# Two attention streams on one core: which bank a maximum is written to, and how many P @ V blocks a run takes

## Chip, core and metric

One core of a Trainium2 chip runs the whole program. The metric is the device time of one execution in microseconds (us). The kernel before was run three times: 1779.37, 1779.55 and 1779.65 us, median 1779.55. One more execution was taken with the hardware profiler: its time is 1779.57 us and its span, from the first to the last profiled instruction, 1777.8 us.

## What is computed

Cut from the reference: `x` is 2048 tokens by 512, there are 32 heads of 16 dimensions, and the second stream is cut into 4 chunks of 512 tokens.

```python
g = sigmoid((x * gate_w).sum(-1, keepdims=True))
# stream A: full softmax attention over all 2048 keys
p = softmax(einsum("bhqd,bhkd->bhqk", q, k) * Dh ** -0.5)
a = einsum("bhqk,bhkd->bhqd", p, v) @ A_wo
# stream B: causal softmax attention inside each chunk of 512, and a memory of the chunks before
for s in range(4):
    p = softmax(einsum("bhqd,bhkd->bhqk", qs, ks) * scale + mask)
    o = gb * (phi(qs) @ M) / (phi(qs) @ z + 1e-6) + (1 - gb) * (p @ vs)
    M, z = M + phi(ks).T @ vs, z + phi(ks).sum()
b = o @ B_wo
out = g * a + (1 - g) * b
```

The softmax subtracts each row's true maximum. So the kernel computes the score products twice: once to find the maxima of the rows (a "maximum"), and once more, with the maximum folded into the product as two more rows of the operands, for the exponentials.

## The kernel before

**Work and slots.** A unit is four heads of one stream against one query chunk: 32 units of A and 32 of B. In the main loop (the `while` loop from line 1019) one slot `n` is one score product of 128 keys by 512 queries; an A unit has 64 slots and a B unit 10 (`SLOTS`, line 29). The units run alternately, A then B, so that a pair has 74 slots, and there are 2368 in all.

In slot `n` the loop issues, in this order: `score_part(n)`, a score product on TensorE into one of three rotating banks of the accumulator memory (tile `st`, L744) and its exponential on ScalarE into a tile `p` (L767, L764); and then `max_part(n + 96)`, the maximum of a slot 96 places later. A maximum of A is one product into one of four banks (tiles `sm0` to `sm3`, L205), read by one VectorE reduction over 512 columns (L226). A maximum of B has, for most of its places, two products side by side in one bank, of 128 and 384 columns or of 256 and 256, and otherwise one of 512. VectorE reads each product of B with an instruction of its own that adds the causal mask (L238, with a short readback behind it). The first of two is read at once; the second waits in the list `rows_left` and is issued by `flush_rows()` when the next maximum comes, behind that one's reduction. The order of VectorE's reads is therefore B first piece, next A, B second piece, while TensorE wrote B, A.

**The bank of a maximum** is `banks[m % 4]` (L1028): the four banks in turn, whatever VectorE has read by then. A product into a bank must wait until the last read of what was there is done.

**Runs.** After every third slot (`BURST = 3`, L31) comes one run on TensorE. It is either three products of an output tile (list `shared`, L913 and L684), where any are pending, or `some_values`, which takes score blocks off a queue and multiplies them with V into the bank `ops` (L801). One block is 128 queries by four heads. Blocks of one group of four that are taken together go out as one wider product (128, 256, 384 or 512 columns); a run that crosses a group makes two. Three slots with their maxima and the run behind them are called a burst below. 74 slots are 24 2/3 bursts, so the runs fall at three different places of the units and the pattern repeats every three units, or 222 slots.

**How many blocks a run takes** is set by `most()` (L1008): normally three (`MOST`), and four when the queue is long. For A the bound falls as the unit nears its end: `64 * (len(queue) - 3) > 11 * left`, where `left` is the unit's blocks that are still to be done. A table `ends` sets the last runs of a unit. A run stops at the end of its unit. When a unit is complete its output tile is due, whose 12 products take the next four runs (`shared`); the blocks that those runs did not take have to be made up.

A pair of row maxima is transposed on TensorE in some bursts (L196, `run_late`), behind the run. The last 94 slots and what follows (`wide`) have a pattern of their own with runs after six slots; there are no maxima left by then.

Of the kernel before, what the change touches and what calls it, by code (L numbers as in the profile page):

```python
# [13 lines left out]
ALU = mybir.AluOpType  # L14
# [8 lines left out]
CH = 512  # L23
# [9 lines left out]
SLOTS = {"A": 64, "B": 10}  # L33
NU = 32
LEAD = 96
BURST = 3
LATER = (2, 3)
MOST = 3
LOW, HIGH = 3, 14
NP = 6  # L40
GAP = {"A": 2, "B": 5}
LATE_T = 9
# [5 lines left out]
def gated_mix(ctx, tc, x, xT, wqkv, a_wo, b_wq, b_wk, b_wv, b_wo, beta, gate_w, out):  # L48
    nc = tc.nc
# [54 lines left out]
    first = {}  # L104
# [5 lines left out]
    nS = len(slots)  # L110
# [64 lines left out]
    tri = {}  # L175
# [3 lines left out]
    def finish_max(u):  # L179
        nm = pmt.pop(u)  # L180
        if u[0] == "A":
            pm, nm = nm, mp.tile([128, 4, 4], F32, tag="nm", name="nm")
            nc.vector.tensor_reduce(nm, pm, axis=AX.X, op=ALU.max, negate=True)  # L183

        ms = mp.tile([128, 2, 2, 2, 4], F32R, tag="ms", name="ms")
        nv = nm.rearrange("p (r h) s -> p r h s", r=2)
        nc.gpsimd.tensor_copy(ms[:, :, 0], nv)  # L187
        nc.gpsimd.tensor_sub(ms[:, :, 1], nv, ms[:, :, 0].bitcast(F32))
        return ms
# [14 lines left out]
    def max_product(ps, u, h, s, n0, n, k, k0=0):  # L204
        nc.tensor.matmul(ps[:, n0:n0 + n], rows(qt[u][:, :, s * 128:(s + 1) * 128], h, 48), rows(k[:, :, k0:k0 + n], h, 48),  # L205
                         start=True, stop=True)

    rows_left = []

    def flush_rows():  # L210
        while rows_left:
            rows_left.pop(0)()

    def max_part(m, bank):

        u, (r, i) = maxs[m]
        side, g, c = u
        if u not in pmt:
            pmt[u] = mp.tile([128, 4, 4] + [4] * (side == "A"), F32, tag="pm" + side, name="pm")
        pm = pmt[u]  # L220
        ps = bank()
        if side == "A":

            kc, s, h = i // 8, i % 8 // 2, 2 * r + i % 2
            max_product(ps, u, h, s, 0, CH, kt_[u, kc])
            nc.vector.tensor_reduce(pm[:, h, s, kc:kc + 1], ps, axis=AX.X, op=ALU.max)  # L226
            flush_rows()
        else:


            k = kt_[u, c]
            mine = [(2 * r + h, s, 128 * (s == 2) + 256 * (s == 1 and h), 128 * (s + 1))
                    for h, s in (((0, 0), (0, 2)), ((0, 1), (1, 1)), ((1, 0), (1, 2)), ((0, 3),), ((1, 3),))[i]]
            for h, s, n0, w in mine:
                max_product(ps, u, h, s, n0, w, k)
            flush_rows()
            for h, s, n0, w in mine:
                rows_left.append(lambda h=h, s=s, n0=n0, w=w: nc.vector.tensor_tensor_reduce(  # L238
                    out=tri["rest"][:, 0:w], in0=ps[:, n0:n0 + w], in1=tri["mask"][:, CH - w:], scale=-1.0, scalar=3.0e38,
                    op0=ALU.add, op1=ALU.min, accum_out=pm[:, h, s:s + 1]))  # L240
            rows_left.pop(0)()
        if m == last_max[u]:
            def finish():

                due = min(e for e in a_last if e >= last_max[u]) + LATE_T
                late.append((min(due, first[u] + LEAD - 12), u, finish_max(u)))
            todo.append((m + 1, finish))
# [15 lines left out]
    def loads(m):  # L263

        m = min(m, len(maxs) - 1)
        while loaded[0] <= m:
            u, (r, i) = maxs[loaded[0]]
            if loaded[0] == first_max[u]:
                load_q(u)
            kc = u[2] if u[0] == "B" else i // 8  # L270
            if (u, kc) not in kt_:
                load_k(u, kc)
            loaded[0] += 1
# [350 lines left out]
    banks = [sm_ps.tile([128, CH], F32, name=f"sm{i}") for i in range(4)]  # L624
# [95 lines left out]
    wide = range(nS - LEAD + 2, nS - 4)  # L720
    assert wide.start % (2 * BURST) == wide.stop % (2 * BURST) == 0

    def from_bank(n):

        return nc.vector.tensor_copy if n > wide.start + 4 else nc.scalar.copy

    queue = []

    def score_part(n):
# [38 lines left out]
        if j % 4 == 3 or j == SLOTS[side] - 1:  # L768
            if side == "B":
# [7 lines left out]
              + [(2, 0, 256), (2, 128, 384)])  # L777

    def some_values(n, most):

        taken = len(queue)
        while queue and most and queue[0][0] <= n:
            _, u, i = queue.pop(0)
            most -= 1
            side, g, c = u
            w = 1
            while (queue and most and queue[0][0] <= n and queue[0][1] == u and (i + w) // 4 == i // 4
                   and (side == "A" or PIECES[i + w][0] == PIECES[i][0])):
                queue.pop(0)
                most -= 1  # L790
                w += 1
            p = pt_[u, i // 4]
            if side == "A":
                c0 = q0 = 128 * (i % 4)
                v = vt[u][:, i // 16, i // 4 % 4]
            else:
                b, c0, q0 = PIECES[i]
                v = vt[u][:, b]
            done = i + w == SLOTS[side]
            for h in range(4):  # L800
                nc.tensor.matmul(ops[32 * h:32 * h + 17, q0:q0 + 128 * w], v[:, 17 * h:17 * h + 17], p[:, h, c0:c0 + 128 * w],  # L801
                                 start=(i == 0), stop=done, tile_position=(0, 32 * h))
            if done:
                raw = ob.tile([128, CH], F32, tag="o", name="oraw")
                from_bank(n)(raw, ops)
                nc.sync.dma_start(od[side, c][4 * g:4 * g + 4].rearrange("h r t -> (h r) t"), raw)
                stored.add(u)
                if side == "B" and c and g % 2 == 0:
                    octet("M", g // 2, c, n + 4)
                if (side, g ^ 1, c) in stored and u != ("A", NG - 1, NCH - 1):  # L810
                    octet(side, g // 2, c, n + (20 if side == "B" and (g < 5 or c < last) else 8))
                if u in between:
                    shared.extend(output(*between[u]))
                if side == "A" and c == 0:
                    shared.extend(later_tile(LATER[g // NO], g % NO))
                break
        return taken - len(queue)
# [117 lines left out]
    def output(c, b, pairs, then, ps=ops):  # L935

        ks = [(os, o, i) for os in pairs for o in os for i in range(2)]
        for k in ks:
            def f(n, k=k):
                os, o, i = k  # L940
                assert loaded_blocks[c, b, os] > len(blocks) - 2
                t = blocks[loaded_blocks[c, b, os] - 1][:, i, o % 2].unsqueeze(1)
                list(products(ps, t, 0, "AB"[i], o, k == ks[0], k == ks[-1]))[n]()
                if k == ks[-1] and n == 2:
                    then(ps, c, b)
            for n in range(3):
                yield lambda n=n, f=f: f(n)
# [57 lines left out]

    ends = {"A": {9: 3, 8: 4, 7: 3, 6: 3, 5: 5}, "B": {10: 3, 7: 3, 4: 4}}

    def most():  # L1008

        if not queue:  # L1010
            return 0
        side = queue[0][1][0]
        left = SLOTS[side] - queue[0][2]
        over = 64 * (len(queue) - LOW) > (HIGH - LOW) * (left if side == "A" else 0)
        return ends[side].get(left, MOST + over)

    filled = [0]
    n = 0
    while n < nS or queue or beside or filled[0] < len(fill):
        for f in beside.pop(n, []):  # L1020
            f()
        if n < nS:
            score_part(n)
        m = n + LEAD
        if m < nS:
            loads(m + PRE)

            max_part(m, lambda: banks[m % 4])  # L1028
        run_todo(m)
        if n >= nS or n % (2 * BURST if n in wide else BURST) == (2 * BURST if n in wide else BURST) - 1:  # L1030
            taken = 0
            if shared:
                for _ in range(3):
                    shared.pop(0)()
            else:
                taken = some_values(n, 8 if n >= nS or n in wide else most())
            if n < 5:


                for i in range(4):  # L1040
                    nc.tensor.matmul(ops[:, 128 * i:128 * i + 128], identf, identf, start=True, stop=True)
            if any(e[0] < m + 1 for e in late):
                run_late(st_ps, "st", m + 1)
            else:

                for _ in range(0 if n >= nS and queue else 4 if n not in wide else 11 - taken if taken < 8 else 0):
                    if filled[0] == len(fill) or fill[filled[0]][0] > n:
                        break
                    fill[filled[0]][1]()
                    filled[0] += 1  # L1050
        n += 1
# [45 lines left out]
```

## Time and profile before

| | |
|---|---|
| median of three runs | 1779.55 us (1779.37 to 1779.65) |
| profiled execution | 1779.57 us, span 1777.8 us |
| TensorE (PE) busy | 1770.5 us, 100% |
| weight loads (PEld) busy | 915.2 us, 51% |
| VectorE (DVE) busy | 1573.5 us, 89% |
| ScalarE (ACT) busy | 1435.4 us, 81% |
| GpSimd (POOL) busy | 641.2 us, 36% |

The projections take the first 302 us or so; the main loop's bursts with maxima run from there to 1702 us; the last stage ends at 1778 us. Matmuls are pipelined and their ends are modelled, so that a matmul which streams behind another still counts as busy: PE at 100% says little by itself. In the rows of the timeline the columns are the start in us, the length in us, the engine, the line, the operation, the tiles written and read, and how many instructions in a row were merged (x8). Where two follow each other with an overlap, the merged length runs from the first start to the last end.

### The profile page before, as it was taken

The numbers are of one execution on the slowest core, as the hardware profiler recorded it, in microseconds if no ns is written. First come the engines' busy times: TensorE is split into PE (matmuls) and PEld (weight loads), VectorE is DVE, ScalarE is ACT, GpSimd is POOL, SyncE is SP. The second block draws the span as 40 slices with busy tenths as digits, with TensorE's granted clock in tenths as the row PEclk, the third lists the DMA queues.
The fourth block names the chain that finished last, engine by engine and source line by source line (L and its number), as shares of the span: only waits on it lengthen the run. The fifth ranks groups of instructions, "written<-read, shape, count | busy, mean of one in ns | idle before, by whom it ended". The sixth has DMA issues, their size and how long they took to land.

```text
span 1777.8 us, 40673 instructions
## 1 busy us (share of the span) xinstructions
PE 1770.5 (100%) x14945; PEld 915.2 (51%) x14945; DVE 1573.5 (89%) x3331; ACT 1435.4 (81%) x2752; POOL 641.2 (36%) x748
## 2 busy tenths in 40 slices
PE   9999999999999999999999999999999999999999
PEld 8887776444444444444444444444444444444444
DVE  4236777999999999999999999999999999999931
ACT  5455445888888888888888888888888888888884
POOL 3002223415161417443434343344434253435343
PEclk9999999999999999999999999999999999999999
DMA  7667566445453536555454544454545353544542
GB/s 251 212 234 239 182 205 187 121 110 134 128 152 107 147 108 179 143 146 128 132 143 121 145 127 146 128 146 126 147 112 154 113 141 116 150 119 138 144 160 62
DMA packets 141270, 261.55 MB, mean 147 GB/s; under 512 B 36328, under 2 KB 58888, under 8 KB 140560
## 3 DMA queue, kind: packets, MB, share of 16 engines
q1 hardware_dynamic: 139712, 257.55, 50.3%
q8 instruction: 119, 1.95, 0.5%
q0 software_dynamic: 1216, 1.14, 0.3%
q14 instruction: 79, 0.65, 0.1%
q10 hardware_dynamic: 144, 0.26, 0.0%
HBM read 174.39 MB, written 83.25 MB: 145 GB/s over the span
## 4 chain that ended last, share of the span: by engine, by line
PE 95%; DVE 1%; ACT 1%; DMA 1%; POOL 1%; issue 0%; SPq 0%; POOLq 0%; DVEq 0%
PE ops L801 33%; PE st L744 27%; PE sm L205 14%; PE pr L311 10%; PE ops L913 4%; PE ops L684 2%; PE sm L913 2%; PE num L514 1%; POOL mn L378 1%; PE pr L401 1%; PE mps L545 0%; DVE pm L226 0%; DMA qdB<-q 0%; PE mt_ps L196 0%; DMA raw<-xT 0%; PE sm L744 0%
## 5 line engine op out<-in xcount | busy, mean ns | idle before, releaser
L767 ACT ACTIVATE p<-st 128x512 f32<-128x512 f32 x2261 | 1189.5, 601 | 152.3 <-PE sm L205 108.2
L226 DVE TENSOR_REDUCE pm<-sm 128x1 f32<-128x512 f32 x2048 | 1281.1, 683 | 11.5 <-PE sm L205 11.3
L744 PE MATMUL st<-qA,kA 50*128 50x512 f32 x2014 | 663.4, 432 | 0.0
L205 PE MATMUL sm<-kA,qA 48*128 48x512 f32 x2048 | 660.4, 428 | 0.4
L801 PE MATMUL ops<-p,vA 128*17 128x128 f32 (+3 forms) x6432 | 552.0, 442 | 0.0
L744 PEld LDWEIGHTS st<-qA,kA 50*128 50x128 f32 x2014 | 328.0, 185 | 415.1 <-ACT p L767 370.6
L205 PEld LDWEIGHTS sm<-kA,qA 48*128 48x128 f32 x2048 | 331.7, 185 | 16.9 <-issue 4.6
L863 POOL TENSOR_TENSOR rcp<-rec,minus 128x32 f32<-128x32 f32 x43 | 234.2, 5446 | 76.4 <-DMA rec<-dend 71.8
L238 DVE CUSTOM_DVE_ANT_0 rest<-sm,mask 128x128 f32<-128x128 f32 (+3 forms) x512 | 247.3, 483 | 1.4
L801 PEld LDWEIGHTS ops<-p,vA 128*17 128x17 f32 x6432 | 130.5, 96 | 214.4 <-issue 189.4
L748 POOL TENSOR_SCALAR_AFFINE_SELECT p<-p 128x512 f32<-128x512 f32 x128 | 79.4, 636 | 324.9 <-ACT p L767 320.4
L205 PE MATMUL sm<-kB,qB 48*128 48x128 f32 (+3 forms) x512 | 166.2, 385 | 0.0
L744 PE MATMUL st<-qB,kB 50*128 50x512 f32 (+1 forms) x495 | 109.3, 330 | 0.3 <-ACT mt L199 0.3
L381 DVE TENSOR_TENSOR q<-full,q 128x512 fp32r<-128x512 f32 x56 | 38.6, 689 | 74.9 <-ACT q L374 67.9
L744 PEld LDWEIGHTS st<-qB,kB 50*128 50x128 f32 x495 | 69.9, 186 | 59.3 <-ACT p L767 48.6
L801 PE MATMUL ops<-p,vB 128*17 128x128 f32 (+3 forms) x1504 | 87.5, 350 | 0.0
L205 PEld LDWEIGHTS sm<-kB,qB 48*128 48x128 f32 x512 | 80.0, 184 | 0.0
L187 POOL CAST ms<-nm 128x16 fp32r<-128x16 f32 x32 | 6.3, 196 | 201.5 <-DVE nm L183 199.6
L378 POOL TENSOR_SCALAR mn<-full 128x512 f32<-128x512 f32 x24 | 36.4, 1515 | 102.5 <-ACT full L373 82.2
L373 ACT COPY full<-pr 128x512 f32<-128x512 f32 x56 | 32.8, 586 | 40.2 <-PE pr L311 37.3
L187 POOL CAST ms<-pm 128x16 fp32r<-128x16 f32 x32 | 6.3, 196 | 127.9 <-DVE pm L238 127.8
L801 PEld LDWEIGHTS ops<-p,vB 128*17 128x17 f32 x1504 | 33.1, 97 | 31.1 <-issue 26.6
(198 smaller groups left out, 1622.7 us busy)
## 6 DMA issues: line engine op xcount, KB each, us to landing
kA<-kdA SPq DMA_DIRECT2D x256, 128.0 KB
vA<-vdA SPq DMA_DIRECT2D x31, 544.0 KB
kA<-kdA SPq DMA_DIRECT2D x256, 64.0 KB
kdA<-q SPq DMA_DIRECT2D x32, 256.0 KB
qdB<-q SPq DMA_DIRECT2D x32, 256.0 KB
qA<-qdA SPq DMA_DIRECT2D x64, 128.0 KB
kdB<-q SPq DMA_DIRECT2D x32, 256.0 KB
qB<-qdB SPq DMA_DIRECT2D x64, 128.0 KB
```

The source lines that it names most:

```text
L205: nc.tensor.matmul(ps[:, n0:n0 + n], rows(qt[u][:, :, s * 128:(s + 1) * 128], h, 48), rows(k[:, :, k0:k0 + n], h, 48), start=True, stop=True)
L226: nc.vector.tensor_reduce(pm[:, h, s, kc:kc + 1], ps, axis=AX.X, op=ALU.max)
L238: rows_left.append(lambda h=h, s=s, n0=n0, w=w: nc.vector.tensor_tensor_reduce(out=tri["rest"][:, 0:w], in0=ps[:, n0:n0 + w], in1=tri["mas ...
L311: nc.tensor.matmul(ps, l(a, k), r(b, k), start=(n == 0), stop=(n == 11))
L378: nc.gpsimd.tensor_scalar_min(ph["mn"], full, 0.0)
L381: nc.vector.tensor_sub(q2, full, q1.bitcast(F32))
L744: nc.tensor.matmul(ps[:, n0:n0 + CH - q0], rows(k[:, :, b * 128:(b + 1) * 128], h, 50), rows(q[:, :, q0:], h, 50), start=True, stop=True)
L748: nc.gpsimd.affine_select(out=x, in_=x, pattern=[[0, 4], [1, 128]], base=0, channel_multiplier=-1, compare_op=ALU.is_ge, fill=0.0)
L767: nc.scalar.activation(p[:, h], ps, AF.Exp, scale=SCALE)
L801: nc.tensor.matmul(ops[32 * h:32 * h + 17, q0:q0 + 128 * w], v[:, 17 * h:17 * h + 17], p[:, h, c0:c0 + 128 * w], start=(i == 0), stop=done ...
L863: eng.tensor_tensor(r, rec, minus, op=ALU.pow)
L913: yield lambda i=i, x=x, w=w: nc.tensor.matmul(ps, t[:, b, x], halved[side][:, o, w], start=start and i == 0, stop=stop and i == 2)
```

## The change

Two things are changed together. First, the bank of a maximum: instead of `banks[m % 4]` the loop takes the bank whose last read stands earliest in VectorE's order. A counter numbers the reads as they are issued, and `oldest()` takes the bank with the lowest number; a read of a second piece of B renews the number of its bank.

Second, `most(n)` decides between three and four blocks from what is left: `runs` is the number of runs up to the place where the unit's last blocks become due, and a run takes four where the blocks left, less four, are at least 3.5 times the runs left, provided that more than six blocks are there to take before the next run (`due`), or that it is the last. For B, and behind the end of a unit, the table `ends` still holds, with four where more than three blocks are queued.

```diff
-LOW, HIGH = 3, 14
+LOW = 3
...
+    read_last = dict(zip(range(4), range(4)))
+    def oldest():
+        return min(read_last, key=read_last.get)
+    def was_read(b):
+        if b is not None:
+            read_last[b] = count[0] = count[0] + 1
+    count = [4]
-    def max_part(m, bank):
+    def max_part(m, bank, b=None):
...
             nc.vector.tensor_reduce(pm[:, h, s, kc:kc + 1], ps, axis=AX.X, op=ALU.max)
+            was_read(b)
             flush_rows()
...
+            if b is not None:
+                read_last[b] = 9 * nS
...
+            def masked(h, s, n0, w):
+                nc.vector.tensor_tensor_reduce(
...
+                was_read(b)
             for h, s, n0, w in mine:
-                rows_left.append(lambda h=h, s=s, n0=n0, w=w: nc.vector.tensor_tensor_reduce(
...
+                rows_left.append(lambda h=h, s=s, n0=n0, w=w: masked(h, s, n0, w))
...
-    def most():
+    def most(n):
         if not queue:
             return 0
-        side = queue[0][1][0]
-        left = SLOTS[side] - queue[0][2]
-        over = 64 * (len(queue) - LOW) > (HIGH - LOW) * (left if side == "A" else 0)
-        return ends[side].get(left, MOST + over)
+        _, u, done = queue[0]
+        side, left = u[0], SLOTS[u[0]] - done
+        runs = (first[u] + SLOTS[side] + GAP[side] + 1 - n) // BURST
+        if side == "B" or runs < 1:
+            return ends[side].get(left, MOST + (len(queue) > LOW))
+        due = min(SLOTS[side], (n + BURST - GAP[side] - first[u] + 1) // 4 * 4) - done
+        return MOST + (left - 4 >= (MOST + 0.5) * runs and (due > 2 * MOST or runs == 1))
...
-            max_part(m, lambda: banks[m % 4])
+            b = oldest()
+            max_part(m, lambda: banks[b], b)
...
-                taken = some_values(n, 8 if n >= nS or n in wide else most())
+                taken = some_values(n, 8 if n >= nS or n in wide else most(n))
```

More of the change, by code (lines that the diff above doesn't have):

```diff
@@ L236, in max_part @@
             flush_rows()
+            def masked(h, s, n0, w):
+                nc.vector.tensor_tensor_reduce(
+                    out=tri["rest"][:, 0:w], in0=ps[:, n0:n0 + w], in1=tri["mask"][:, CH - w:], scale=-1.0, scalar=3.0e38,
+                    op0=ALU.add, op1=ALU.min, accum_out=pm[:, h, s:s + 1])
+                was_read(b)
             for h, s, n0, w in mine:
-                rows_left.append(lambda h=h, s=s, n0=n0, w=w: nc.vector.tensor_tensor_reduce(
-                    out=tri["rest"][:, 0:w], in0=ps[:, n0:n0 + w], in1=tri["mask"][:, CH - w:], scale=-1.0, scalar=3.0e38,
-                    op0=ALU.add, op1=ALU.min, accum_out=pm[:, h, s:s + 1]))
+                rows_left.append(lambda h=h, s=s, n0=n0, w=w: masked(h, s, n0, w))
             rows_left.pop(0)()
```

## The prediction

> **What bounds the kernel now.** I read the busy times by stage first, then the timeline of VectorE, then that of TensorE. One window is 222 slots, three units of each stream; the fence has two of them.
>
> ```profile
> core 0: us, PE busy (x) PEld busy (x) DVE busy (x) ACT busy (x) POOL busy (x), PEclk, DMA share, GB/s
> ...
> 889.64:1026.28 136.64, 136.64 (x1283) 63.00 (x1286) 136.45 (x292) 120.88 (x235) 51.71 (x59) 1.00 0.50 136
> ...
> 1436.20:1572.85 136.65, 136.65 (x1284) 63.05 (x1286) 136.49 (x292) 120.91 (x235) 51.71 (x59) 1.00 0.52 136
> ```
>
> VectorE is busy for 136.45 of 136.64 us, and ScalarE for 120.88. TensorE's 136.64 says little, since a matmul that streams behind another counts as busy. VectorE's own busy time hides something too, which its timeline shows.
>
> ```profile
> 860.25 4.87 DVE L226 TENSOR_REDUCE pm<-sm 128x1 f32<-128x512 f32 x8
> 865.11 0.69 DVE L238 CUSTOM_DVE_ANT_0 rest<-sm,mask 128x512 f32<-128x512 f32 x1
> 865.73 0.08 DVE L238 DVE_READ_ACCUMULATOR2_ANT pm<- 128x1 f32 x1
> 865.73 1.28 DVE L226 TENSOR_REDUCE pm<-sm 128x1 f32<-128x512 f32 x2
> 867.00 0.69 DVE L238 CUSTOM_DVE_ANT_0 rest<-sm,mask 128x512 f32<-128x512 f32 x1
> ...
> 867.62 9.31 DVE L226 TENSOR_REDUCE pm<-sm 128x1 f32<-128x512 f32 x15
> 876.84 0.21 DVE L183 TENSOR_REDUCE nm<-pm 128x16 f32<-128x64 f32 x1
> 876.97 3.07 DVE L226 TENSOR_REDUCE pm<-sm 128x1 f32<-128x512 f32 x5
> 880.13 0.29 DVE L238 CUSTOM_DVE_ANT_0 rest<-sm,mask 128x128 f32<-128x128 f32 x1
> 880.35 0.08 DVE L238 DVE_READ_ACCUMULATOR2_ANT pm<- 128x1 f32 x1
> ...
> 882.83 0.55 DVE L238 CUSTOM_DVE_ANT_0 rest<-sm,mask 128x384 f32<-128x384 f32 x1
> 883.30 0.08 DVE L238 DVE_READ_ACCUMULATOR2_ANT pm<- 128x1 f32 x1
> ...
> 887.49 0.42 DVE L238 CUSTOM_DVE_ANT_0 rest<-sm,mask 128x256 f32<-128x256 f32 x1
> 887.83 0.08 DVE L238 DVE_READ_ACCUMULATOR2_ANT pm<- 128x1 f32 x1
> ...
> 890.66 4.40 DVE L226 TENSOR_REDUCE pm<-sm 128x1 f32<-128x512 f32 x7
> ```
>
> Eight reductions take 4.87 us and two take 1.28. So the step from one to the next is (4.87 - 1.28) / 6 = 0.598 us, one alone takes 1.28 - 0.60 = 0.68, and each overlaps the one before it by 0.08 us. A delay of less than 0.08 us between two reads leaves no idle time in any view; it shows only as a group longer than its steps. The 15 reductions from 867.62 should take 14 x 0.598 + 0.68 = 9.05 us and take 9.31: 0.26 us were lost. The seven at 890.66 should take 4.27 and take 4.40: 0.13 lost.
>
> VectorE's work in a window, at its own pace: 192 reductions x 0.598 = 114.8 us; B's masked reads by width, from the starts of the reads and their readbacks, 0.21, 0.34, 0.47 and 0.62 us (880.13 to 880.35, 887.49 to 887.83, 882.83 to 883.30, 865.11 to 865.73), four of each for a unit, three units, 19.7 us; the small reduction at 876.84 takes 0.13 before the next starts, three times, 0.4 us. Sum 134.9. The window lasts 136.64, so about 1.7 us of it, 1.3%, is VectorE waiting for TensorE. That is all the change can win back here: 9.8 windows lie between 360 and 1702 us, 17 us in all.
>
> **Where it is lost.** TensorE's bursts, first score to first score:
>
> ```profile
> 868.31 0.50 PE L744 MATMUL st<-qA,kA 50*128 50x512 f32 x1
> ...
> 870.20 0.50 PE L744 MATMUL st<-qA,kA 50*128 50x512 f32 x1
> ...
> 872.08 0.50 PE L744 MATMUL st<-qA,kA 50*128 50x512 f32 x1
> ...
> 873.76 0.49 PE L744 MATMUL st<-qA,kA 50*128 50x512 f32 x1
> ...
> 875.66 0.50 PE L744 MATMUL st<-qA,kA 50*128 50x512 f32 x1
> ```
> ```profile
> 925.39 0.50 PE L744 MATMUL st<-qA,kA 50*128 50x512 f32 x1
> ...
> 927.22 0.39 PE L196 MATMUL mt_ps<-identf,ms 128*32 128x128 f32 x4
> 927.54 0.50 PE L744 MATMUL st<-qA,kA 50*128 50x512 f32 x1
> ...
> 929.25 0.50 PE L744 MATMUL st<-qA,kA 50*128 50x512 f32 x1
> ...
> 931.05 0.49 PE L744 MATMUL st<-qA,kA 50*128 50x512 f32 x1
> ```
>
> A burst with a run of four blocks takes 1.89 us (868.31 to 870.20), with three blocks 1.68 (872.08 to 873.76), with four in two products 1.90 (873.76 to 875.66), with four and the transposed maxima 2.15 (925.39 to 927.54). VectorE needs 3 x 0.598 = 1.79 us for three reads of A, and with a B among them 1.82 (0.62 + 1.20) or 1.88 (two pieces, 0.68 + 1.20). So beside A alone a four makes TensorE 0.10 us later and a three 0.11 earlier; beside a B a four costs 0.01 to 0.07 and a three gains 0.14 to 0.20. TensorE has a reserve of a few tenths, since the banks are filled ahead; a row of fours eats it, and then each further one is lost time on VectorE.
>
> I followed `most()` through the loop slot by slot, for the old and the new rule. The runs of an A unit behind the four shared runs and the three of B (T: with transposed maxima):
>
> old: I 4444444 3 444 3T33 444; II 4344433443444T332 44; III 443444344434 3T433 2 4
> new: I 444444444 3 4 3T33 444; II 443434343434 3T433 44; III 443434343434 3T4343 4
>
> Each sums to 64 blocks. I, II and III are the three places at which runs fall in a unit. The rows above are of a unit I: the delays at 865.11 and 867.00 (0.08 and 0.07 against the 0.598 steps before them) and the 0.26 stand in its seven fours, the 0.17 ahead of 880.13 (876.97 + 5 x 0.598 = 879.96) at its T, the 0.13 of 890.66 behind its last three. Sum 0.71. For II and III:
>
> ```profile
> 912.10 10.32 DVE L226 TENSOR_REDUCE pm<-sm 128x1 f32<-128x512 f32 x17
> ...
> 927.38 0.68 DVE L226 TENSOR_REDUCE pm<-sm 128x1 f32<-128x512 f32 x1
> 928.13 0.29 DVE L238 CUSTOM_DVE_ANT_0 rest<-sm,mask 128x128 f32<-128x128 f32 x1
> ```
> ```profile
> 958.10 9.93 DVE L226 TENSOR_REDUCE pm<-sm 128x1 f32<-128x512 f32 x16
> 967.94 0.21 DVE L183 TENSOR_REDUCE nm<-pm 128x16 f32<-128x64 f32 x1
> 968.07 4.27 DVE L226 TENSOR_REDUCE pm<-sm 128x1 f32<-128x512 f32 x7
> 972.34 0.29 DVE L238 CUSTOM_DVE_ANT_0 rest<-sm,mask 128x128 f32<-128x128 f32 x1
> ```
>
> II loses 0.07 in its 17 reductions (10.25 at their pace) and 0.15 ahead of 928.13, behind the four with a T: 0.22. III loses 0.28 in 16 (9.65) and 0.08 ahead of 972.34: 0.36. These rows name 1.29 of the 1.7; the other 0.4 is in spots of some 0.05 each.
>
> **The change part by part.** *The runs.* Unit I gets two more fours in its row: 2 x 0.10 = 0.20 lost more. Ahead of its T there is now a 3 and a 4 in place of a 3 and three fours, 0.20 less, against the 0.17 lost there; I take 0.07 saved, as its reserve starts from nothing. I: 0.13 worse (bounds 0 and 0.20). Unit II alternates fours and threes, +0.10 and -0.11, so the reserve stays, and its T stands behind a three, 0.21 us shorter: all 0.22 is saved. Unit III alternates too: 0.28 and half of the 0.08, 0.32 saved. Of the unnamed 0.4 I take a quarter, 0.10 (bounds 0 and 0.4). Sum -0.13 + 0.22 + 0.32 + 0.10 = 0.51 a window, times 9.8: **5.0 us**. There are 9 fewer products of A in all (804 and 795 pieces); by 1.89 against 1.90 that is 0.1 us, nothing. The queue gets up to two blocks longer at some places, so that a `p` tile is released a run later; ScalarE's idle time covers that (120.88 of 136.64 busy). If that cover were gone, the next exponential, and through its score bank the next score, would stand a run late.
>
> *The banks.* What differs is the order behind a B of two pieces: the next burst's second maximum no longer waits for the second piece, its third does, at the same moment as the second did. One spot a window shows such a wait in full:
>
> ```profile
> 980.40 0.50 PE L205 MATMUL sm<-kB,qB 48*128 48x256 f32 x2
> 980.74 0.40 PE L744 MATMUL st<-qB,kB 50*128 50x512 f32 x1
> 981.13 0.50 PE L205 MATMUL sm<-kA,qA 48*128 48x512 f32 x2
> ```
> ```profile
> PEld st L744 <- ACT p L767: 419.3, 809, 0.9
> ...
> PEld sm L205 <- DVE pm L238: 4.0, 13, 0.5
> ```
>
> The product at 981.13 could stand beside the score at 980.74: 0.39 us. It comes where TensorE is ahead, and the whole list names 4.0 us of such waits against 419.3 for ScalarE's score banks, which take over as the limit. So between 0 and 0.39 a window; nearer to 0, since reserve that TensorE gains while it is ahead is used only by the next row of fours: 0.04, **0.4 us** in all. Behind the moved wait stand the burst's third product, its run and the next score; they waited there already. The counter and the choice are made when the program is built, no engine runs them; DMAs, SP's and POOL's queues keep their order.
>
> Forecast: 1779.57 - 5.0 - 0.4 = **1774.2 us** against the profiled execution's own time, of which 1.8 lies around the span; the median of the runs is 0.02 less, so nothing is to be converted. Its own range, by the bounds of I and of the unnamed spots, is 1770 to 1776.5.
>
> **The rivals.**
>
> *More is won.* The banks free TensorE behind each two-piece B, and the whole 0.39 becomes reserve that unit I uses: another 0.35 x 9.8 = 3.4 us, 1770.8. For it: unit I's losses are still there to win. Against it: the 419.3 us of the score banks.
>
> *VectorE is full.* What looks like lost steps is the reads' own scatter, and only the idle 0.19 us of a window (136.64 - 136.45) can be won: 1.9 us, 1777.7, not to be told from no change. For it: the busy share. Against it: the groups of 4.87 and of 9.31 have the same step but for the fours beside them. The Trainium skill, Perfetto Trace Analysis, Identifying the Most-Contended Engine, says that occupancy is a fair measure of VectorE's closeness to its limit; by that rule the time would be this one, and the overlapping groups of the trace speak against it. To this case I add the one that delays only move along, from II and III into the next unit's start.
>
> *Slower: the threes don't repay.* A three that waits for a score bank gains nothing: 929.25 to 931.05 is one of 1.80 us. If the threes between the fours are all like this, a pair costs 1.89 + 1.80 against 3.59, 0.10 lost, six pairs each in II and III: 1.2 a window, in place of the 0.58 that II and III lose by the rows above. Worse by 0.62 x 9.8 = 6.1 us, 1785.7. It decides from a mean of 1.70 us for these threes (3.59 - 1.89). Against it: the three behind a row of fours took 1.68.
>
> **How the numbers follow.** What a measurement here can tell from no change is 0.2%, 3.6 us: faster is below 1776.0. Chances: forecast 0.52, more won 0.16, VectorE full 0.23, threes don't repay 0.09. Faster takes the second whole and most of the first, 0.64; same the 0.23 and the forecast's upper end, 0.27; slower 0.09. The range 1769 to 1779.5 holds the first three cases but for their edges; the slower one is left out.
>
> **What would show it.** Each window shorter by about 0.5 us; in units II and III groups of reductions at the 0.598 step, with no 9.93 for 16; in unit I the long group of its fours longer than today's by 0.2 us. The wait at 981.13 gone. It is wrong if the threes in II and III take 1.75 us or more, or if unit I's row costs more than II and III give back.

## The result and the profile after

The changed kernel takes 1772.95 us (median of six runs, 1772.17 to 1773.54); the kernel before, run beside it, 1779.72 us (1779.37 to 1781.19). The ratio is 0.9961, with an interval of 0.9951 to 0.9971: faster by 6.8 us. The profiled execution has a span of 1771.8 us; before it was 1777.8.

One window of 222 slots in the timeline by stretches, from the first maximum of one unit I to that of the next; columns as before:

```profile
core 0: us, PE busy (x) PEld busy (x) DVE busy (x) ACT busy (x) POOL busy (x), PEclk, DMA share, GB/s
855.11:991.02 135.91, 135.91 (x1277) 62.32 (x1274) 135.87 (x292) 120.88 (x235) 58.93 (x67) 1.00 0.49 136
```

The same work takes 135.9 us where it took 136.6. VectorE's 134.9 us of work are unchanged, so it now waits 1.0 us and not 1.7. VectorE's timeline of the changed kernel, units I, II and III one after the other (the reduction is at L238 now and the masked read at L253):

```profile
858.39 4.87 DVE L238 TENSOR_REDUCE pm<-sm 128x1 f32<-128x512 f32 x8
...
865.73 9.50 DVE L238 TENSOR_REDUCE pm<-sm 128x1 f32<-128x512 f32 x15
...
875.27 3.07 DVE L238 TENSOR_REDUCE pm<-sm 128x1 f32<-128x512 f32 x5
878.26 0.28 DVE L253 CUSTOM_DVE_ANT_0 rest<-sm,mask 128x128 f32<-128x128 f32 x1
...
888.79 4.28 DVE L238 TENSOR_REDUCE pm<-sm 128x1 f32<-128x512 f32 x7
...
910.09 10.25 DVE L238 TENSOR_REDUCE pm<-sm 128x1 f32<-128x512 f32 x17
...
920.39 3.67 DVE L238 TENSOR_REDUCE pm<-sm 128x1 f32<-128x512 f32 x6
924.06 0.29 DVE L253 CUSTOM_DVE_ANT_0 rest<-sm,mask 128x128 f32<-128x128 f32 x1
...
955.75 9.66 DVE L238 TENSOR_REDUCE pm<-sm 128x1 f32<-128x512 f32 x16
...
965.45 4.29 DVE L238 TENSOR_REDUCE pm<-sm 128x1 f32<-128x512 f32 x7
969.76 0.29 DVE L253 CUSTOM_DVE_ANT_0 rest<-sm,mask 128x128 f32<-128x128 f32 x1
```

Read against the step of 0.598 us: in unit I, whose run of fours has become nine long, the 15 reductions take 9.50 and not 9.31, at their own pace 9.05; the loss there has grown from 0.26 to 0.45 us. The 0.17 ahead of the masked read is gone (875.27 + 5 x 0.598 = 878.26) and the 0.13 in the seven reductions too (4.28). In units II and III the 17 and the 16 now run at their own pace, 10.25 and 9.66 (before 10.32 and 9.93). What is left there stands ahead of a masked read, in the burst behind whose run the maxima are transposed: 0.08 us at 924.06 and 0.12 at 969.76.

To compare kernels I summed, for every read of VectorE, by how much it starts later than the one before it and that one's step allow (lateness above 0.012 us, mean of eight windows). The sum moves by some 0.03 us with the step that is taken as the base. The same sum for the kernel before, the changed one and eight of the nine experiments:

| kernel | lateness in a window, us | median, us | ratio to before |
|---|---|---|---|
| before | 1.48 | 1779.7 | |
| changed | 0.85 | 1772.95 | 0.9961 (0.9951 to 0.9971) |
| banks alone | 1.14 | 1775.8 | 0.9979 (0.9970 to 0.9988) |
| runs alone | 1.07 | 1775.4 | 0.9975 (0.9966 to 0.9984) |
| fours first | 2.64 | 1792.3 | 1.0070 (1.0056 to 1.0084) |
| unit I spread | 0.96 | 1773.9 | 0.9966 (0.9953 to 0.9978) |
| transposes later | 1.50 | 1784.8 | 1.0028 (1.0016 to 1.0041) |
| aligned | 1.89 | 1787.0 | 1.0040 (1.0028 to 1.0053) |
| aligned, B first in a burst | 0.95 | 1775.5 | 0.9975 (0.9965 to 0.9985) |
| aligned, no B in the short burst | 0.63 | 1770.5 | 0.9951 (0.9937 to 0.9965) |

### The profile page after: what moved, and what is told of

Same layout as the page of the kernel before. It is cut to its first block, busy times and chain, and to the rows that moved or that the text cites. A ratio compares the mean times of both kernels' runs of the same rounds, so it can differ in the third digit from the quotient of the medians.

```text
span 1771.8 us, 40530 instructions
## 1 busy us (share of the span) xinstructions
PE 1764.5 (100%) x14873; PEld 910.4 (51%) x14873; DVE 1568.3 (89%) x3331; ACT 1435.0 (81%) x2752; POOL 641.1 (36%) x748
## 3 DMA queue, kind: packets, MB, share of 16 engines
q0 software_dynamic: 1216, 1.14, 0.3%
## 4 chain that ended last, share of the span: by engine, by line
PE 96%; DVE 1%; DMA 1%; ACT 1%; POOL 1%; issue 0%; SPq 0%; POOLq 0%; DVEq 0%
PE ops L820 33%; PE st L763 27%; PE sm L205 14%; PE pr L330 10%; PE ops L932 4%; PE ops L703 2%; PE sm L932 2%; PE num L533 1%; POOL mn L397 1%; PE pr L420 1%; PE mps L564 0%; DMA qdB<-q 0%; PE mt_ps L196 0%; DMA raw<-xT 0%; PE sm L763 0%; DVE jk L492 0%
## 5 line engine op out<-in xcount | busy, mean ns | idle before, releaser
L238 DVE TENSOR_REDUCE pm<-sm 128x1 f32<-128x512 f32 x2048 | 1278.6, 683 | 11.3 <-PE sm L205 11.2
L205 PE MATMUL sm<-kA,qA 48*128 48x512 f32 x2048 | 668.9, 426 | 0.2
L763 PE MATMUL st<-qA,kA 50*128 50x512 f32 x2014 | 656.7, 431 | 0.0
L820 PE MATMUL ops<-p,vA 128*17 128x256 f32 (+3 forms) x6360 | 552.3, 445 | 0.0
L205 PEld LDWEIGHTS sm<-kA,qA 48*128 48x128 f32 x2048 | 338.8, 185 | 12.3 <-issue 4.6
L253 DVE CUSTOM_DVE_ANT_0 rest<-sm,mask 128x128 f32<-128x128 f32 (+3 forms) x512 | 247.0, 482 | 0.4
L763 PE MATMUL st<-qB,kB 50*128 50x512 f32 (+1 forms) x495 | 105.3, 329 | 0.3 <-ACT mt L199 0.3
L898 POOL TENSOR_TENSOR v<-v,inv 128x512 f32<-128x512 f32 x31 | 39.9, 1286 | 24.5 <-DMA inv<-rdA 20.7
```

What stands on the lines that cost most here:

```text
L253: nc.vector.tensor_tensor_reduce(out=tri["rest"][:, 0:w], in0=ps[:, n0:n0 + w], in1=tri["mask"][:, CH - w:], scale=-1.0, scalar=3.0e38, op ...
L763: nc.tensor.matmul(ps[:, n0:n0 + CH - q0], rows(k[:, :, b * 128:(b + 1) * 128], h, 50), rows(q[:, :, q0:], h, 50), start=True, stop=True)
L898: eng.tensor_mul(k["v"], k["v"], k["inv"])
```

## The experiments

**The two parts alone.** One kernel keeps the new banks and has the old rule in `most(n)`, the other has the new rule with the banks in turn. The lines that begin with `#` name the runs.

```diff
 # e1_banks_only: the old rule for the runs
-        runs = (first[u] + SLOTS[side] + GAP[side] + 1 - n) // BURST
...
-        return MOST + (left - 4 >= (MOST + 0.5) * runs and (due > 2 * MOST or runs == 1))
+        over = 64 * (len(queue) - LOW) > (14 - LOW) * (left if side == "A" else 0)
+        return ends[side].get(left, MOST + over)
 # e2_runs_only
-            b = oldest()
-            max_part(m, lambda: banks[b], b)
+            max_part(m, lambda: banks[m % 4])
```

> The new choice of banks with the old rule for the runs. By the prediction's sum the banks are worth 0.4 us: 1779.3 us, with the wait for a bank behind a two-piece B gone and the groups of 15 and 16 reductions as long as before (9.31 and 9.93 us). The rival (the banks free TensorE behind each two-piece B and that becomes reserve, 0.39 us a window) gives 3.8 us: 1775.9 us, with the losses behind those places gone and the ones in the rows of fours smaller.

> The new rule for the runs with the banks in turn. By the prediction's sum the runs are worth 5.0 us: 1774.7 us, with the alternating units at the 0.598 us step. If the two parts add up, this gain and that of the banks alone make 6.8 us together. The rival (the banks carried most of it) gives 1776.5 us or more.

The banks alone gave 1775.8 us, 3.9 less than the kernel before beside them; the runs alone 1775.4, 4.3 less. The rival was right on the banks: they are worth ten times what the sum gave them. Together they would be 8.2, and the changed kernel won 6.8: some of the lateness is won by either. By place in the window (lateness in us, mean of eight windows):

| place | before | banks | runs | both |
|---|---|---|---|---|
| I, third and fourth four | 0.13 | 0.05 | 0.13 | 0.12 |
| I, eighth and ninth four | 0 | 0 | 0.16 | 0.16 |
| I, burst of the transposes | 0.17 | 0.17 | 0 | 0 |
| I, last three fours | 0.10 | 0.00 | 0.10 | 0 |
| II, behind 3 444 | 0.08 | 0.10 | 0 | 0 |
| II, burst of the transposes and the next | 0.21 | 0.21 | 0.09 | 0.09 |
| III, its rows of fours | 0.25 | 0.18 | 0.01 | 0.01 |
| third of the shared runs behind II and behind III | 0.10 | 0.00 | 0.10 | 0.01 |

For the most part, each has its own places. The runs clear the rows of fours in II and III; the banks clear the ends of the units and what comes behind them. Two places are alike in all four kernels: some 0.19 us in the fifth to seventh four of unit I, and 0.12 in the third of the shared runs behind it. VectorE's groups of 15, 17 and 16 with the banks alone, and the 15 and the seven of unit I with the runs alone:

```profile
866.25 9.31 DVE L238 TENSOR_REDUCE pm<-sm 128x1 f32<-128x512 f32 x15
...
910.69 10.34 DVE L238 TENSOR_REDUCE pm<-sm 128x1 f32<-128x512 f32 x17
...
956.61 9.88 DVE L238 TENSOR_REDUCE pm<-sm 128x1 f32<-128x512 f32 x16
```
```profile
866.42 9.49 DVE L238 TENSOR_REDUCE pm<-sm 128x1 f32<-128x512 f32 x15
...
889.48 4.40 DVE L238 TENSOR_REDUCE pm<-sm 128x1 f32<-128x512 f32 x7
```

How the banks bring so much shows in a burst that the prediction did not go into, in unit I, with a run of three blocks behind it. TensorE's matmuls and then its weight loads, in the kernel before:

```profile
883.08 0.49 PE L744 MATMUL st<-qA,kA 50*128 50x512 f32 x1
883.09 0.50 PE L205 MATMUL sm<-kA,qA 48*128 48x512 f32 x1
883.42 0.40 PE L744 MATMUL st<-qA,kA 50*128 50x512 f32 x1
883.44 0.61 PE L205 MATMUL sm<-kA,qA 48*128 48x512 f32 x2
883.78 0.40 PE L744 MATMUL st<-qA,kA 50*128 50x512 f32 x1
884.11 0.84 PE L801 MATMUL ops<-p,vA 128*17 128x384 f32 x8
884.88 0.50 PE L744 MATMUL st<-qA,kA 50*128 50x512 f32 x1
```
```profile
883.08 0.18 PEld L205 LDWEIGHTS sm<-kA,qA 48*128 48x128 f32 x1
883.19 0.19 PEld L744 LDWEIGHTS st<-qA,kA 50*128 50x128 f32 x1
883.44 0.26 PEld L205 LDWEIGHTS sm<-kA,qA 48*128 48x128 f32 x2
883.55 0.19 PEld L744 LDWEIGHTS st<-qA,kA 50*128 50x128 f32 x1
```

And the same burst with the banks alone, whose runs are the same:

```profile
881.73 0.49 PE L763 MATMUL st<-qA,kA 50*128 50x512 f32 x1
881.74 0.72 PE L205 MATMUL sm<-kA,qA 48*128 48x512 f32 x2
882.07 0.62 PE L763 MATMUL st<-qA,kA 50*128 50x512 f32 x2
882.30 0.40 PE L205 MATMUL sm<-kA,qA 48*128 48x512 f32 x1
882.63 0.84 PE L820 MATMUL ops<-p,vA 128*17 128x384 f32 x8
883.40 0.50 PE L763 MATMUL st<-qA,kA 50*128 50x512 f32 x1
```
```profile
881.74 0.29 PEld L205 LDWEIGHTS sm<-kA,qA 48*128 48x128 f32 x2
881.84 0.50 PEld L763 LDWEIGHTS st<-qA,kA 50*128 50x128 f32 x2
882.16 0.18 PEld L205 LDWEIGHTS sm<-kA,qA 48*128 48x128 f32 x1
```

The second maximum's matmul stands 0.02 us late before, at 883.44 where its score stands at 883.42: that is all that the matmuls show of its wait. But it is the weight load that waits. With the bank free, it starts 0.11 us behind the first (two loads of 0.18 in the 0.29 us from 881.74); with the bank still to be read (the readback of its last read, shown above at 883.30, ends at 883.38) it goes at 883.44, and the third score's load behind it only at 883.55. The third score then starts 0.36 us behind the second (883.78) and not 0.23 (the two from 882.07 take 0.62 us, one alone 0.39), and the burst takes 1.80 us and not 1.67. A wait of 0.02 us costs 0.13. It is so throughout: in nine windows from 473 us on, this burst takes 1.78 to 1.80 us before and 1.66 to 1.68 with the banks alone. The prediction's spot at 981.13 has its counterpart too: 2.38 us to the next burst before, 2.16 with the banks alone.

```profile
980.40 0.49 PE L744 MATMUL st<-qB,kB 50*128 50x512 f32 x1
...
982.78 0.44 PE L744 MATMUL st<-qB,kB 50*128 50x384 f32 x1
```
```profile
978.83 0.49 PE L763 MATMUL st<-qB,kB 50*128 50x512 f32 x1
...
980.99 0.44 PE L763 MATMUL st<-qB,kB 50*128 50x384 f32 x1
```

**Fours first.** If the order of threes and fours is what decides, taking all fours first must cost.

```diff
-        return MOST + (left - 4 >= (MOST + 0.5) * runs and (due > 2 * MOST or runs == 1))
+        return MOST + (left - 4 >= MOST * runs and (due > 2 * MOST or runs == 1))
```

> The changed kernel, but a run takes four blocks for as long as the blocks left are above three for each run left, so that all units begin with ten to twelve fours in a row and end with threes and ones; the same 64 blocks a unit. If a row of fours eats TensorE's reserve and each further one costs 0.10 us beside A, units II and III lose some 0.45 us each more: 0.9 us a window, 9 us in all, 1782 us. If only the number of blocks counts and not their order, 1773 us.

It took 1792.3 us, with the fewest products of all kernels and the most lateness. Its groups of 15, 17 and 16 all lose 0.43 to 0.44 us against their own pace of 9.05, 10.25 and 9.65. The row of fours eats the reserve, and the cost is more than the 9 us expected: the units' ends, where the reserve is gone, lose as well.

```profile
873.01 9.49 DVE L238 TENSOR_REDUCE pm<-sm 128x1 f32<-128x512 f32 x15
...
918.14 10.68 DVE L238 TENSOR_REDUCE pm<-sm 128x1 f32<-128x512 f32 x17
...
964.86 10.09 DVE L238 TENSOR_REDUCE pm<-sm 128x1 f32<-128x512 f32 x16
```

**Unit I spread.** Is unit I's loss that of its nine fours in a row, or is TensorE short of time in the whole unit?

```diff
-        return MOST + (left - 4 >= (MOST + 0.5) * runs and (due > 2 * MOST or runs == 1))
+        return MOST + (left - 4 >= (MOST + (0.75 if first[u] % 222 == 0 else 0.5)) * runs and (due > 2 * MOST or runs == 1))
```

> The changed kernel, but in unit I the nine fours in a row are spread: 4 3 444 3 444 3 4 4 4 3 444, the same 64 blocks in the same 17 runs; units II and III as changed. If unit I is bound by TensorE from end to end, because it has a run less, its 0.55 us stay and only move to the later runs: 1773 us. If the row of fours itself is the cost, about 0.4 us a window are won: 1769 us.

1773.9 us. The 15 reductions lose 0.23 in place of 0.45, and the seven at the unit's end lose 0.23 where they lost nothing:

```profile
865.62 9.28 DVE L238 TENSOR_REDUCE pm<-sm 128x1 f32<-128x512 f32 x15
...
888.68 4.50 DVE L238 TENSOR_REDUCE pm<-sm 128x1 f32<-128x512 f32 x7
```

The loss moves and stays. Unit I has 24 bursts for the same 64 + 10 blocks and 12 products that II and III do in 25, and TensorE is short of time in it in both orders that were run.

**Aligned runs.** So the runs were put at the same places of every unit: after every third slot of the 74 and after the last two, 25 a unit.

```diff
+    def run_at(n):
+        return n % 74 % BURST == BURST - 1 or n % 74 == 73
...
-        runs = (first[u] + SLOTS[side] + GAP[side] + 1 - n) // BURST
+        runs = sum(run_at(i) for i in range(n, first[u] + SLOTS[side] + GAP[side] + 1))
...
-        if n >= nS or n % (2 * BURST if n in wide else BURST) == (2 * BURST if n in wide else BURST) - 1:
+        if n >= nS or (n % (2 * BURST) == 2 * BURST - 1 if n in wide else run_at(n)):
```

> The changed kernel, but the runs fall at the same places of every unit: after every third slot of the 74, and after the last two, so 25 runs for each unit in place of 24, 25 and 25. By the theory that unit I loses its 0.6 us because it has a run less and so nine fours in a row, all units now alternate fours and threes and the 0.6 us of each window is won: about 5 us, 1768 us. The rival: the one run more in three units and the masked reads, which now fall at other places of the burst, cost as much as they bring: 1773 us or more.

1787.0 us: slower than before. The 16 reductions of unit III run at their pace, and unit I loses 0.19 us in place of 0.63. But B's maxima are placed for bursts that begin at a multiple of three, and now stand second or last in two units of three. VectorE's timeline, with its idle time and what ended it in brackets:

```profile
943.32 0.69 DVE L238 TENSOR_REDUCE pm<-sm 128x1 f32<-128x512 f32 x1 [0.71 <-PE sm L205]
...
960.09 9.65 DVE L238 TENSOR_REDUCE pm<-sm 128x1 f32<-128x512 f32 x16
...
974.71 0.69 DVE L238 TENSOR_REDUCE pm<-sm 128x1 f32<-128x512 f32 x1 [0.45 <-PE sm L205]
```

A B that stands last in its burst has its short first read done before the run behind it is, and VectorE waits for the next burst. That is only a part of the 7.3 us by which this kernel is slower than the one before: its windows are 136.87 us long and not 136.64, which makes 2.3 us in all (the sum of latenesses, with its threshold, would make 4.0). Another 2.8 lie in the last unit of A that has maxima (54.4 us from the last reduction of the unit of A before it to its own, 51.6 in the kernel before), and 1.7 behind the last reduction of all.

So the maxima of B were put at the first slot of the new bursts, and then also out of the burst of two slots, with the last unit's runs counted as in the changed kernel:

```diff
         while len(at_) < 10 * len(bs):
             at_.append(at_[-1] + apart[len(at_) % 2])
+        if 1 < k < NU - 1:
+            starts = [m for m in range(len(maxs) + 6, len(maxs) + 74) if (m - LEAD) % 74 % 3 == 0]
+            at_ = [starts[i] for i in (0, 1, 4, 5, 8, 9, 12, 13, 16, 18)]   # e5_aligned_b
+            at_ = [starts[i] for i in (0, 1, 4, 5, 10, 11, 14, 15, 18, 19)]   # e9_aligned_c, in its place
...
+        if u == ("A", (NU - 2) % NG, (NU - 2) // NG):   # e9_aligned_c only
+            runs = (first[u] + SLOTS[side] + GAP[side] + 1 - n) // BURST
```

> The run places aligned to every unit as in e4_aligned, and the maxima of B put at the first slot of those bursts. By the theory that e4_aligned was slow only because B's reads stood inside or at the end of a burst in two units of three (0.79 and 0.53 us lost at two places of a window, and 0.2 us lost in the unit where they stood first), all units lose about 0.2 us: 0.6 a window in place of the changed kernel's 0.85, 2.5 us, 1770.5 us. If the one run more is what costs, it stays above 1780 us.

> As e5_aligned_b, but no maximum of B in the burst of two slots at the end of a unit (where e5_aligned_b lost 0.23 to 0.27 us in each unit, 0.7 of its 0.95 us a window), and the last units' runs as in the changed kernel (e5_aligned_b's end was 1.7 us longer). If those two places are all that aligning costs, a window loses 0.2 to 0.3 us in place of the changed kernel's 0.85, 6 us less in all: 1767 us. If the lateness only moves to the next two-piece B, the time stays at 1773 us or above.

The first took 1775.5 us, with 0.95 us of lateness in a window, 0.73 of it at the B behind the short burst. Not all of that is TensorE's: a masked read stands there directly behind the readback of another, 0.227 us behind it in each unit, and the last experiment shows such a pair 0.12 us apart with nothing late. So 0.35 of a window's 0.95 is VectorE's own. The second took **1770.5 us** (1770.05 to 1771.73), below all runs of the changed kernel: a version that beats both. Of its 5.0 us against the first, 3.1 lie in the windows (135.60 and 135.92 us long) and 1.8 behind the last reduction. Its lateness is 0.63 a window and not 0.2 to 0.3: about 0.2 us a unit stay behind the burst of two slots, whose shared run is as long as behind three while VectorE's work is a read shorter. The 12 reductions of a unit's row of threes and fours are at their pace (11 x 0.598 + 0.68 = 7.26), the 12 across the short burst 0.15 above:

```profile
865.99 7.26 DVE L241 TENSOR_REDUCE pm<-sm 128x1 f32<-128x512 f32 x12
...
886.80 7.41 DVE L241 TENSOR_REDUCE pm<-sm 128x1 f32<-128x512 f32 x12
```

**Transposes later.** What is left in II and III stands in the bursts of the transposes. Is it theirs?

```diff
-LATE_T = 9
+LATE_T = 15
```

> The changed kernel with the transposed maxima due six slots later, so that they stand in a burst of A alone, two bursts behind their present one. The 0.09 and 0.10 us that units II and III lose ahead of the masked read there are 1.9 us in all. If they come from the transposes standing just ahead of a two-piece B, the time falls to 1771.5 us or so; if the transposes cost their 0.26 us wherever they stand, it is 1773 us or more.

1784.8 us, a miss for both. The transposes of an A and a B unit, which went together, now stand in two bursts, 3 and 6 slots later in I and II (in III one keeps its place). The lateness ahead of II's masked read stays, 0.09 us, without them, so it is not theirs.

The trace has another candidate. The first masked read of a B unit waits for GpSimd as well as for TensorE, and one of the two waits is an instruction of its own on VectorE's queue, 0.105 us ahead of the read. In the changed kernel this read is late in 18 units, and it then starts 0.147 us behind the end of its B's second product (here 923.92, the read 924.06). The same read of a later B of two pieces, which waits for TensorE alone, starts 0.037 us behind that end where it is late (9 of them). The difference, 0.11 us, would be all of the lateness in II and most of it in III. No run took that wait away, so it is not shown. In the aligned kernel of 1770.5 us these products are done 0.4 us ahead, and the reads are not late.

```profile
923.37 0.55 PE L205 MATMUL sm<-kB,qB 48*128 48x128 f32 x2
```

The transposes now cost what the unit's ends had in reserve: 0.24 us at the end of unit I, where the seven reductions take 4.50 us, 0.15 at that of II and 0.25 at that of III. From the changed kernel's 0.85 to 1.50 us a window it is 6.4 us in 9.8 windows. The other half lies behind the last maximum: from the last reduction to the end of the span it is 80.9 us, in the changed kernel 75.8. Why the end became longer was not followed up.

**Both pieces read at once.** The other way to bring reads and banks into one order is to read B's second piece right behind the first, in the kernel before.

```diff
-            rows_left.pop(0)()
+            flush_rows()
```

> The kernel before, with its banks in turn and its runs, but both pieces of a B maximum read at once, ahead of the next A's reduction; reads and banks are then in one order. If the mismatch of the two orders is what the new choice of banks removes, the 0.4 us wait behind two-piece Bs goes here too, and the time comes near that of the banks alone: 1775.8 us. If the choice of banks brings its gain another way, it stays at 1779.7 us or above.

1795.1 us, and it does not tell what it was meant to tell, since it makes VectorE itself slower:

```profile
887.52 0.08 DVE L238 DVE_READ_ACCUMULATOR2_ANT pm<- 128x1 f32 x1
887.64 0.56 DVE L238 CUSTOM_DVE_ANT_0 rest<-sm,mask 128x384 f32<-128x384 f32 x1
888.12 0.08 DVE L238 DVE_READ_ACCUMULATOR2_ANT pm<- 128x1 f32 x1
888.12 1.28 DVE L226 TENSOR_REDUCE pm<-sm 128x1 f32<-128x512 f32 x2
```

Behind a readback a reduction starts in the same hundredth (888.12), but another masked read only 0.12 us later (887.52 to 887.64). In the trace that second read waits for a semaphore which VectorE itself raises with the readback; both write the tile `rest`. Whether the wait or the kind of instruction costs the 0.12 us was not tested. Eighteen such pairs in a window make 2.2 us, 21 us in all, more than the 14.9 by which the kernel is slower than the one before beside it (1780.2 us; ratio 1.0085, 1.0071 to 1.0099).

## Why the prediction was right, and where it was not

The time, 1772.95 us against a forecast of 1774.2, and the direction were right: 6.8 us against 5.4. Of the two terms of the sum one was right in its mechanism and nearly in its size, and the other was several times too small. By its own steps:

*VectorE's hidden lateness is what can be won* held: by the table, 0.63 us less in a window times 9.8 windows is 6.2 of the 6.8 us, and the kernels stand in the order of their lateness but for the one with aligned runs and B first in a burst, whose end is 1.8 us longer (77.6 us from the last reduction on, 75.8 in the changed kernel). With the transposes later and with aligned runs the time is longer than the lateness alone makes it, for the ends named above. The rival that VectorE is full fell with it: VectorE was busy for 136.45 of 136.64 us and had 1.7 us to give. By the rule of the Trainium skill (Perfetto Trace Analysis, Identifying the Most-Contended Engine) that share is a fair measure of how near it is to its limit. In this case's trace the share is 1.1% too high, and this 1.1% is what the change was about.

*The runs* were sized well in II and III: 0.22 and 0.32 were forecast, and the 17 and the 16 reductions did come to their pace. At unit I's transposes 0.07 saved was taken, and all 0.17 was saved; the two fours more cost 0.16 to 0.19 against 0.20. So unit I came out about even, where 0.13 worse was forecast. The 0.15 behind II's transposes went; the 0.08 ahead of III's masked read, half of which was to go, is 0.12, and II has 0.08 of the same kind (924.06). The 0.10 taken from the unnamed spots did not come: the places in the table make up 0.45 us, more than the 0.41 by which the runs alone shorten the lateness of a window. In time the runs alone brought 4.3 us against 5.0.

*The banks* are the step that was mis-sized: "nearer to 0", 0.04 a window and 0.4 us in all. They bring 3.9 us alone, and 2.4 on top of the runs (1775.4 to 1772.95). Alone they reach the upper bound, 0.39 us a window or 3.8 in all, and on top of the runs they lie within it; what failed is the choice near 0. The bound itself came from elsewhere than the gain does: the wait was priced by how late the matmul stood, 0.39 us at one place, and the places where it stood 0.02 late were left out; and the 4.0 us in the list of waits count only idle time of the weight loads. The rival that more is won priced the banks at 3.8 us, and its mechanism, that the time becomes reserve which the next fours use, fits the places in the table; most of the gain, 0.20 of 0.34 us, stands at the units' ends and directly behind them. That the runs brought less than forecast and the banks more is why the total came out near, and that is luck.

*The threes don't repay* fell. In II and III of the changed kernel the 73 threes between fours take 1.66 to 1.68 us, 1.67 on the mean, where this rival needed 1.70 and more. The first scores of three bursts show a three (905.29 to 906.96) and a four beside a B (to 908.88):

```profile
905.29 0.50 PE L763 MATMUL st<-qA,kA 50*128 50x512 f32 x1
...
906.96 0.50 PE L763 MATMUL st<-qA,kA 50*128 50x512 f32 x1
...
908.88 0.49 PE L763 MATMUL st<-qA,kA 50*128 50x512 f32 x1
```

The burst of 1.80 us at 929.25 that it was argued from stands directly behind a two-piece B, and with the banks alone it takes 1.72, so that most of what it had above 1.67 was a wait for a bank of the maxima.

*The nine products less* were put at nothing, and no run speaks against it: the kernel with fours first has 208 products of A fewer than the changed one and is the slowest but one.

## What to carry to other kernels

Where two engines are near balance, compare the length of groups of back-to-back instructions with their step; an overlap of 0.08 us hid 1% of the time from every busy share here. Look then at the order of long and short work on the feeding engine and not only at its sum: here the same blocks in another order went from 1773 to 1792 us. And where buffers are released in another order than they are filled, try giving them out by the order of release and not in turn; here that was worth 3.9 us of 1780.

## What was not expected of the hardware

A bank that comes free 0.02 us late made a burst 0.13 us longer (1.80 against 1.67), as the weight load waits for it and the loads behind it follow only then. A masked read that waits for the readback of another, directly ahead of it on VectorE, starts 0.12 us behind that readback, and a plain reduction starts at once. And a late masked read that waits for two engines starts 0.147 us behind the products, one that waits for TensorE alone 0.037.
